# Pooled attention and squared-ReLU feed-forward on one core: chunk 1's softmax in another layout, another weight conversion, and split products in half of chunk 0

## The chip, the cores and the metric

The kernel runs on one NeuronCore of a Trainium2 chip. Its inputs lie in the chip's memory (HBM) and its result is written there. The metric is the device time of one execution in microseconds (us). The engines named below are PE (TensorE: matmuls and transposes by a matmul with an identity; PEld is its weight loading), DVE (VectorE), ACT (ScalarE), POOL (GpSimd) and SP (SyncE, which here only issues DMAs). Each engine works through its own queue in order.

## The reference

Keys and values are pooled over 8 tokens, each of the 8 batches and 8 heads attends over 72 pooled tokens, and the result, seen as 4608 tokens of width 512, goes through two weight matrices with a squared ReLU between them.

```python
def _attn_ref(q, k, v):                       # 8 batches, 8 heads, 576 tokens, head size 64
    k_p = k.reshape(B, H, Sp, 8, D).mean(axis=3)          # Sp = 72
    v_p = v.reshape(B, H, Sp, 8, D).mean(axis=3)
    scores = scale * np.matmul(q, k_p.transpose(0, 1, 3, 2))
    scores = scores - np.max(scores, axis=-1, keepdims=True)
    attn = np.exp(scores)
    attn = attn / (np.sum(attn, axis=-1, keepdims=True) + 1e-09)
    return np.matmul(attn, v_p).astype(np.float32)
...
    x = attn_out.transpose(0, 2, 1, 3).reshape(B * S, H * D)     # 4608 x 512
    h = np.maximum(x @ w_in, 0.0)                                # 512 x 2048
    return (h * h @ w_out).astype(np.float32)                    # 2048 x 512
```

The two weight matrices come as 64-bit floats, q, k and v as 32-bit floats.

## The kernel before

The 4608 tokens are cut into 12 chunks of 384 (`CH`), numbered c. Chunk 0 lies within batch 0; chunk 1 takes 192 tokens from batch 0 and 192 from batch 1 (`segments`). For each chunk there are 16 steps, one for each block of 128 columns of the hidden layer (`fc`). `hidden(c, fc)` multiplies the chunk's attention output x by a block of w_in (tile `h`), `project(c, fc)` multiplies the squared ReLU by a block of w_out and sums over all 16 blocks in three PSUM banks (tile `o`). `project` runs two steps behind `hidden` (`LAG`).

Products are made in one of two ways. From chunk 1 on every operand is split into a high and a low part in the type fp32r (`split`: ACT rounds to the high part, DVE subtracts), and three products of such parts replace one product of 32-bit floats: 12 matmuls for a block of `h`. In chunk 0 the weights are not yet split, and plain 32-bit floats are multiplied: 4 matmuls for a block of `h`, and the trace shows two records for each.

The weights are converted on the chip from the two 32-bit words of a 64-bit float. One weight piece (`key`, 512 KB of 64-bit values) is loaded into a `raw` tile by `land`. `magnitude` lets ACT take the absolute value of the high words into a half tile `wf`. `to_float32` then lets DVE do four instructions on 128x512 elements for each key: a clamp, a shift with a mask, and two that bring in sign and low bits. `split_weights` later makes the split pair `wt` for chunk 1 and all that follow. There are 32 keys.

Attention goes by pairs of heads p (four pairs a chunk). `transpose_q` turns q (tile `qps`, copied to `st`), `scores` multiplies with the pooled keys (tile `sps`, copied to `sc`). In chunk 1 and later the scores lie with the 72 pooled tokens on the partitions, so maximum and sum run across partitions: GpSimd does them with `partition_all_reduce` (tiles `mx` and `tot`), the sums travel to HBM and back (`send_sums`, `fetch_sums`), DVE inverts them, and the reciprocals travel once more (`rd`, `rb`). `weigh_values` multiplies with the pooled values (tile `av`). Chunk 0 is done with the tokens on the partitions: `token_scores`, `token_normalise` (DVE reductions, tiles `tm` and `te`) and `token_turn`, which transposes the weights back (tile `pps`).

Before step 0 stands a part written out by hand: it pools the keys of batches 0 and 1 (`pool_k`), pools values with a matmul against a matrix of ones (`pool_v_pair`, tile `vps`, copied to `vp`), and does all of chunk 0's attention. After it, the table `work` says which function runs in which step; `at(step, f, ...)` fills it. `EARLY` holds the steps for chunk 1's pairs, `STEADY` for the later ones. In a step the order is: `hidden`, the PE part of that step's attention functions, `project`, then the rest for ACT and DVE, the weight conversions, and last the activation of the `h` block just made. All DMAs are issued by SP in program order; each one also waits on one of eight semaphores taken in turn, so that a DMA is issued only when the eighth one before it has landed.

Three PSUM banks (`ps_a`) serve the tiles `qps`, `sps`, `kps`, `vps` and `av`; two (`ps_h`) serve `h`, and three (`ps_o`) the sums `o`.

Of the kernel before, what the change touches and what calls it, by code (L numbers as in the profile page):

```python
# [10 lines left out]
F32 = mybir.dt.float32  # L11
F32R = mybir.dt.float32r
U32 = mybir.dt.uint32
AF = mybir.ActivationFunctionType
ALU = mybir.AluOpType
AX = mybir.AxisListType
EXP_MIN = 2.0 ** -15
EXP_MAX = 122879.9921875
# [14 lines left out]
def pooled_attn_relu2_ffn(  # L33
# [38 lines left out]
    IDLE = (3, 1)  # L72
# [9 lines left out]
    EARLY = ((-19, -16, -13, -10), (0, 2, 3, 5, 5, 6, 7, 8))  # L82
# [14 lines left out]
    make_identity(nc, ident)  # L97
# [43 lines left out]
    def magnitude(key):  # L141

        words = raw[key].rearrange("p a (n w) -> p a n w", w=2)
        wf[key] = half_tile("f", "wf_" + "_".join(map(str, key)))
# [112 lines left out]
    def pool_v_pair(b, p):  # L257
# [6 lines left out]
        def then():  # L264
            DVE.tensor_copy(kv[b][2][:, 2 * p:2 * p + 2, :].rearrange("s h d -> s (h d)"), pt[:SP_, :2 * D])
# [49 lines left out]
    def scores(c, p):  # L315
# [3 lines left out]
        early = c == 1  # L319
        if early:  # L320

            blocks = st.rearrange("p (i t s) -> p i t s", i=2, s=QT)
            for i in range(2):
                h = 2 * p + i
                for t, (b, _, _) in enumerate(segments(c)):
                    for two in range(2):
                        rows = slice(two * D, (two + 1) * D)
                        PE.matmul(ss[two][:SP_, (i * 2 + t) * QT:(i * 2 + t + 1) * QT], lhsT=kf[b][rows, h // KH, h % KH * SP_:(h % KH + 1) * SP_],
                                  rhs=blocks[rows, i, t, :], start=True, stop=True)
        else:  # L330
# [374 lines left out]
```

## Time and profile before

| | us |
|---|---|
| median of 3 runs (lowest, highest) | 972.17 (971.12, 972.57) |
| the profiled execution | 971.68 |
| its span, first to last instruction | 969.9 |
| PE busy (98% of the span) | 946.1 |
| DVE busy (65%) | 628.5 |
| ACT busy (44%) | 428.3 |
| POOL busy (41%) | 394.1 |

The time is the span plus 1.8 us around it. Times of day in this text (such as "at 43.83") are us from the start of the span. In the rows of the timeline the first number is the start, the second how long the group lasted up to its last end; since matmuls overlap, the pace of PE is read from one start to the next. In the rows of the stages the number ahead of the comma is the length of the stage, and then come busy time and count for each engine.

### The profile page before, as it was taken

The numbers are of one execution on the slowest core, as the hardware profiler recorded it, in microseconds if no ns is written. First come the engines' busy times: TensorE is split into PE (matmuls) and PEld (weight loads), VectorE is DVE, ScalarE is ACT, GpSimd is POOL, SyncE is SP. The second block draws the span as 40 slices with busy tenths as digits, with TensorE's granted clock in tenths as the row PEclk, the third lists the DMA queues.
The fourth block names the chain that finished last, engine by engine and source line by source line (L and its number), as shares of the span: only waits on it lengthen the run. The fifth ranks groups of instructions, "written<-read, shape, count | busy, mean of one in ns | idle before, by whom it ended". The sixth has DMA issues, their size and how long they took to land.

```text
span 969.9 us, 13344 instructions
## 1 busy us (share of the span) xinstructions
PE 946.1 (98%) x4888; PEld 793.5 (82%) x4888; DVE 628.5 (65%) x1034; ACT 428.3 (44%) x847; POOL 394.1 (41%) x209
## 2 busy tenths in 40 slices
PE   5989899999999999999999999999999999999998
PEld 5644457888888888888888888888888888888997
DVE  4869997877765556767775656667776555453221
ACT  1644466774434445344444434443543434432322
POOL 4288733544344443443434335343534534440000
PEclk9999999999999999999999999999999999999999
DMA  9926212112211112112112102102311210100000
GB/s 239 365 95 217 82 34 66 48 52 87 60 45 62 38 38 70 34 51 92 54 39 76 37 20 78 52 30 52 95 52 30 77 32 18 58 10 9 33 1 32
DMA packets 53361, 64.45 MB, mean 66 GB/s; under 512 B 14936, under 2 KB 34480, under 8 KB 53296
## 3 DMA queue, kind: packets, MB, share of 16 engines
q1 hardware_dynamic: 53296, 63.61, 21.4%
q8 instruction: 38, 0.62, 0.3%
q14 instruction: 27, 0.22, 0.1%
HBM read 53.87 MB, written 9.71 MB: 66 GB/s over the span
## 4 chain that ended last, share of the span: by engine, by line
PE 85%; DVE 8%; issue 3%; DMA 2%; ACT 1%; POOL 0%; SPq 0%; DVEq 0%; POOLq 0%
PE o L29 38%; PE h L29 37%; PE av L29 4%; PE sps L29 3%; DVE wf_o L29 2%; DVE wf_i L29 2%; PE qps L29 1%; PE vps L29 1%; DMA q<-in_q_dram 1%; DMA rd<-rr 0%; DVE st L29 0%; PE kps L29 0%; DVE sc L29 0%; DVE kp L29 0%; POOL tot L29 0%
## 5 line engine op out<-in xcount | busy, mean ns | idle before, releaser
L29 PE MATMUL h<-xh,w_i 128*128 128x384 f32 x1408 | 389.1, 337 | 0.0
L29 POOL PARTITION_ALL_REDUCE tot<-sc x88 | 250.1, 2889 | 217.8 <-issue 201.6
L29 PE MATMUL o<-w_o,gh 128*128 128x512 f32 x1056 | 335.2, 398 | 0.4 <-ACT ob L29 0.4
L29 PEld LDWEIGHTS h<-xh,w_i 128*128 128x128 f32 x1408 | 258.7, 188 | 8.5 <-issue 0.5
L29 PE MATMUL h<-xl,w_i 128*128 128x384 f32 x704 | 238.0, 338 | 0.0
L29 PEld LDWEIGHTS o<-w_o,gh 128*128 128x128 f32 x1056 | 192.6, 188 | 52.1 <-issue 15.3
L29 POOL PARTITION_ALL_REDUCE mx<-sc x88 | 131.4, 1540 | 243.6 <-ACT sc L29 243.6
L29 DVE TENSOR_TENSOR gl<-r,gh 128x384 fp32r<-128x384 f32 x176 | 146.5, 832 | 108.4 <-ACT gh L29 106.5
L29 PE MATMUL o<-w_o,gl 128*128 128x512 f32 x528 | 208.7, 395 | 0.0
L29 DVE TENSOR_TENSOR r<-r 128x384 f32<-128x384 f32 x160 | 105.7, 661 | 108.7 <-ACT r L29 108.3
L29 ACT CAST gh<-r 128x384 fp32r<-128x384 f32 x176 | 90.4, 514 | 150.1 <-DVE r L29 149.6
L29 PEld LDWEIGHTS h<-xl,w_i 128*128 128x128 f32 x704 | 132.2, 188 | 8.1 <-issue 0.7
L29 ACT ACTIVATE r<-h 128x384 f32<-128x384 f32 x192 | 93.8, 488 | 99.9 <-PE h L29 98.6
L29 PEld LDWEIGHTS o<-w_o,gl 128*128 128x128 f32 x528 | 99.1, 188 | 22.5
L29 DVE TENSOR_TENSOR st<-qps,st 64x384 fp32r<-64x384 f32 x80 | 60.3, 754 | 48.1 <-ACT st L29 47.2
L29 ACT CAST st<-qps 64x384 fp32r<-64x384 f32 x80 | 59.4, 742 | 52.6 <-PE qps L29 52.0
L29 ACT ACTIVATE sc<-sc 72x384 f32<-72x384 f32 x88 | 43.7, 525 | 70.1 <-DVE sc L29 70.1
L29 ACT CAST xh<-rb 128x384 fp32r<-128x384 f32 x44 | 22.6, 513 | 108.5 <-DVE rb L29 108.5
L29 DVE TENSOR_REDUCE vp<-v 72x64 f32<-72x512 f32 x48 | 51.0, 1063 | 0.0
L29 DVE TENSOR_REDUCE kp<-k 96x64 f32<-96x512 f32 x42 | 43.7, 1041 | 3.4 <-DMA k<-in_k_dram 3.4
L29 DVE TENSOR_TENSOR sc<-sc,mx 72x384 f32<-72x384 f32 x88 | 44.6, 546 | 0.0
L29 PE MATMUL av<-sc,vp 72*64 72x384 f32 (+1 forms) x256 | 43.1, 425 | 0.9 <-ACT sc L29 0.9
(82 smaller groups left out, 701.8 us busy)
## 6 DMA issues: line engine op xcount, KB each, us to landing
k<-in_k_dram SPq DMA_DIRECT2D x48, 192.0 KB
out_dram<-ob SPq DMA_DIRECT2D x36, 256.0 KB
rb<-rd SPq DMA_DIRECT2D x88, 96.0 KB
raw_i<-in_moe_w_in_dram SPq DMA_DIRECT2D x16, 512.0 KB
raw_o<-in_moe_w_out_dram SPq DMA_DIRECT2D x16, 512.0 KB
v<-in_v_dram SPq DMA_DIRECT2D x48, 144.0 KB
q<-in_q_dram SPq DMA_DIRECT2D x30, 192.0 KB
q<-in_q_dram SPq DMA_DIRECT2D x32, 96.0 KB
```

Of the source, the lines that this page charges most:

```text
L29: return lambda *a, **k: self.tc.keep_in_program_order(f(*a, **k))
```

## The change

It has several parts, all of which concern the time before step 0, chunk 0 and the attention of chunk 1:

- `EARLY`: chunk 1's softmax is done like chunk 0's, with `token_scores`, `token_normalise` and `token_turn`. For chunk 1 the exponentials are read by ACT straight from PSUM, in eight instructions a pair, each with its own bias.
- Weights: ACT also converts a 16-bit part of the low word into the bits to be added, in place in the `raw` tile, and DVE does three instructions a key.
- `SPLIT = 8`: blocks 0 to 7 of chunk 0 use plain products as before; blocks 8 to 15 use split parts of x (`split_x0`) and split w_in, whose `split_weights` moves into chunk 0.
- The identity for transposes is built by DVE with ramps and comparisons (before: by GpSimd). `keep_busy` issues 16 matmuls before the first transposes and 2 later (before: 3 and 1).
- The copies of `vps` go from DVE to ACT.
- The loads are reordered, and batch 1's value pairs 2 and 3, the transposes of batch 1's keys and chunk 1's first q and scores move from the part ahead of step 0 into steps 0 to 3.

```diff
-EXP_MIN = 2.0 ** -15
-EXP_MAX = 122879.9921875
+SHIFT = 2.0 ** 16
+EXP_MIN = 2.0 ** -15 * SHIFT
+EXP_MAX = 122879.9921875 * SHIFT
+LOW = 7.4999 / 65535
...
-    IDLE = (3, 1)
+    IDLE = (16, 2)
...
-    FIRST, EAGER, AHEAD = 2, 8, 5
+    FIRST, EAGER, AHEAD = 2, 10, 4
+    SPLIT = 8
...
-    EARLY = ((-19, -16, -13, -10), (0, 2, 3, 5, 5, 6, 7, 8))
+    EARLY = ((-16, -13, -10, -7), (0, 1, 2, 3, 4))
...
-    make_identity(nc, ident)
+    ramp = const.tile([P, 2, 32], F32, name="ramp")
+    DVE.memset(ident, 0.0)
+    DVE.memset(ramp[:, 0, :1], 0.0)
+    for n in (1, 2, 4, 8, 16):
+        DVE.tensor_scalar(ramp[:, 0, n:2 * n], ramp[:, 0, :n], float(n), None, op0=ALU.add)
+    DVE.transpose(ramp[:, 1, :], ramp[:, 0, :])
+    for n in range(0, P, 32):
+        rows = slice(n, n + 32)
+        DVE.tensor_scalar(ident[rows, rows], ramp[rows, 0, :], ramp[rows, 1, :1], None, op0=ALU.is_equal)
...
-        ACT.activation(wf[key].rearrange("p (a n) -> p a n", a=2), words[..., 1].bitcast(F32), AF.Abs)
+        ACT.activation(wf[key].rearrange("p (a n) -> p a n", a=2), words[..., 1].bitcast(F32), AF.Abs, scale=SHIFT)
+        halves = raw[key].bitcast(U16).rearrange("p a (n w) -> p a n w", w=4)
+        ACT.activation(words[..., 0], halves[..., 1], AF.Copy, scale=LOW)
...
             DVE.tensor_scalar(m, m, EXP_MIN, EXP_MAX, op0=ALU.max, op1=ALU.min)
-        for _, _, m in parts:
-            DVE.tensor_scalar(m, m, 3, 0x3FFFFFF8, op0=ALU.logical_shift_left, op1=ALU.bitwise_and)
         for words, _, m in parts:
-            DVE.scalar_tensor_tensor(m, words[..., 1], 0xC0000000, m, op0=ALU.bitwise_and, op1=ALU.bitwise_or)
+            DVE.scalar_tensor_tensor(m, m, 3, words[..., 0], op0=ALU.logical_shift_left, op1=ALU.bitwise_or)
         for words, _, m in parts:
-            DVE.scalar_tensor_tensor(m, words[..., 0], 29, m, op0=ALU.logical_shift_right, op1=ALU.bitwise_or)
+            DVE.scalar_tensor_tensor(m, words[..., 1], 0x80000000, m, op0=ALU.bitwise_and, op1=ALU.bitwise_or)
...
-            DVE.tensor_copy(kv[b][2][:, 2 * p:2 * p + 2, :].rearrange("s h d -> s (h d)"), pt[:SP_, :2 * D])
+            ACT.copy(kv[b][2][:, 2 * p:2 * p + 2, :].rearrange("s h d -> s (h d)"), pt[:SP_, :2 * D])
...
     def token_scores(c, p):
-        ss = [ps_o.tile([P, 512], F32, name=f"sps_{c}_{p}_{j}", tag=f"o{(2 * p + j) % NTT}") for j in range(2)]
+        ss = token_banks(c, p, "sps", "o")
...
+                if c:
+                    DVE.tensor_scalar(m[:, 1, i], m[:, 0, i], -SCALE, None, op0=ALU.mult)
...
+                for t in range(NQ if c else 0):
+                    ACT.activation(e[i][:, t], views[i][:, t], AF.Exp, bias=m[:, 1, i, t:t + 1], scale=SCALE)
...
+    def split_x0():
+        xts[0] = [sb.tile([P, NPAIR, CH], F32R, name=f"{x}_0", tag=x, bufs=2) for x in ("xh", "xl")]
+        for i, x in enumerate(x0):
+            split(*(t[:, 2 * i:2 * i + 2] for t in xts[0]), x)
...
-            if c == 0:
-                prods += [(wf[key][:, cols], xts[c][:, cc, :])]
+            if c == 0 and fc < SPLIT:
+                prods += [(wf[key][:, cols], x0[cc // 2][:, cc % 2, :])]
             else:
                 prods += [(wt[key][:, w, cols], xts[c][x][:, cc, :]) for w, x in ((0, 0), (0, 1), (1, 0))]
...
+    load_q(1, 0)
...
-    for key in first_keys:
+    for key in keys[:FIRST + 2]:
         land(key)
+    for p in range(NPAIR):
+        load_v_pair(1, p)
...
-        after = [token_scores(0, p + 2)] if p + 2 < NPAIR else []
-        after.append(pool_v_pair(1, p))
+        after = [token_scores(0, p + 2), pool_v_pair(1, p)] if p + 2 < NPAIR else []
...
-        transpose_k(1, hf)()
+        at(0, transpose_k, 1, hf)
         at(9 + hf, split_k, 1, hf)
+    for p in range(2, NPAIR):
+        at(p, pool_v_pair, 1, p)
+    at(3, split_x0)
...
-        at(14 + int(i * 0.48), split_weights, key, DVE)
+        if key[0] == "i" and key[1] * WC >= SPLIT * P:
+            at(need[key] + 1, split_weights, key, DVE)
+        else:
+            at(14 + int(i * 0.48), split_weights, key, DVE)
```

The first place where the order changes is SP's queue ahead of step 0. Before, batch 1's values (`vv_0` to `vv_3`, the second set) follow the last keys of batch 1 (`k_4`) at once:

```order
L29 DMA k_4_95<-in_k_dram 96x512 x2
L29 DMA vv_0_96<-in_v_dram 96x2x384
L29 DMA vv_1_97<-in_v_dram 96x2x384
L29 DMA vv_2_98<-in_v_dram 96x2x384
L29 DMA vv_3_99<-in_v_dram 96x2x384
L29 DMA raw_i_0_100<-in_moe_w_in_dram 128x2x512
L29 DMA raw_i_2_101<-in_moe_w_in_dram 128x2x512
L29 DMA raw_o_102<-in_moe_w_out_dram 128x1024
L29 DMA raw_i_0_103<-in_moe_w_in_dram 128x2x512
```

In the changed kernel, on the same queue, two loads of chunk 1's q and four weight pieces stand between them:

```order
L34 DMA k_4_104<-in_k_dram 96x512 x2
L34 DMA q_0_105<-in_q_dram 96x2x128 x2
L34 DMA raw_i_0_106<-in_moe_w_in_dram 128x2x512
L34 DMA raw_i_2_107<-in_moe_w_in_dram 128x2x512
L34 DMA raw_o_108<-in_moe_w_out_dram 128x1024
L34 DMA raw_i_0_109<-in_moe_w_in_dram 128x2x512
L34 DMA vv_0_110<-in_v_dram 96x2x384
L34 DMA vv_1_111<-in_v_dram 96x2x384
L34 DMA vv_2_112<-in_v_dram 96x2x384
L34 DMA vv_3_113<-in_v_dram 96x2x384
```

Six DMAs moved ahead of `vv_0`, and nothing else in that stretch.

The second place is PE ahead of step 0. Before, the four poolings of batch 1's values (`vps` from the second `vv` set), the `pps` transposes and the `av` products alternate down to the keys of batch 1 (`kps`):

```order
L29 MATMUL vps_1_356<-vv_1_97,ones 72x128 x6
L29 MATMUL av_0_364<-sc_0_328,vp_154 64x384 x2
L29 MATMUL pps_1_0_368<-ident,te_1_228 72x96 x4
L29 MATMUL pps_1_1_369<-ident,te_1_228 72x96 x4
L29 MATMUL vps_2_396<-vv_2_98,ones 72x128 x6
L29 MATMUL av_1_403<-sc_1_378,vp_154 64x384 x2
L29 MATMUL pps_2_0_410<-ident,te_2_332 72x96 x4
L29 MATMUL pps_2_1_411<-ident,te_2_332 72x96 x4
L29 MATMUL vps_3_430<-vv_3_99,ones 72x128 x6
L29 MATMUL av_2_437<-sc_2_420,vp_154 64x384 x2
L29 MATMUL pps_3_0_441<-ident,te_3_382 72x96 x4
L29 MATMUL pps_3_1_442<-ident,te_3_382 72x96 x4
```

In the changed kernel the same stretch of PE goes on to the first block `h_0` without poolings 2 and 3:

```order
L34 MATMUL vps_1_387<-vv_1_111,ones 72x128 x6
L34 MATMUL av_0_396<-sc_0_359,vp_186 64x384 x2
L34 MATMUL pps_1_0_400<-ident,te_1_259 72x96 x4
L34 MATMUL pps_1_1_401<-ident,te_1_259 72x96 x4
L34 MATMUL av_1_428<-sc_1_410,vp_186 64x384 x2
L34 MATMUL pps_2_0_437<-ident,te_2_363 72x96 x4
L34 MATMUL pps_2_1_438<-ident,te_2_363 72x96 x4
L34 MATMUL av_2_456<-sc_2_447,vp_186 64x384 x2
L34 MATMUL pps_3_0_460<-ident,te_3_414 72x96 x4
L34 MATMUL pps_3_1_461<-ident,te_3_414 72x96 x4
L34 MATMUL av_3_479<-sc_3_470,vp_186 64x384 x2
L34 MATMUL h_0_514<-x_0_394,wf_i_0_432 128x384 x2
```

Two poolings left the stretch; `vps_0` and `vps_1` stay where they were, ahead of `pps_0` and of `av_0`.

The third place is ACT behind the last copy of x (`x_363`, now `x_1_395`). Before, the keys, the q and two weight pieces follow:

```order
L29 COPY x_363<-av_3_463 128x384
L29 COPY kf_467<-kps_0_468 128x288
L29 COPY kf_467<-kps_1_473 128x288
L29 COPY st_0_489<-qps_0_484 128x384
L29 ACTIVATE wf_o_495<-raw_o_102 128x512
L29 ACTIVATE wf_o_495<-raw_i_0_103 128x512
L29 COPY sc_0_512<-sps_0_0_502 72x2x192
```

In the changed kernel, behind the same copy on ACT, ten weight instructions come first:

```order
L34 COPY x_1_395<-av_3_479 128x384
L34 ACTIVATE wf_o_483<-raw_o_108 128x512
L34 ACTIVATE raw_o_108<-raw_o_108 128x512
L34 ACTIVATE wf_i_0_486<-raw_i_0_109 128x512
L34 ACTIVATE raw_i_0_109<-raw_i_0_109 128x512
L34 ACTIVATE wf_i_0_486<-raw_i_2_114 128x512
L34 ACTIVATE raw_i_2_114<-raw_i_2_114 128x512
L34 ACTIVATE wf_o_483<-raw_o_115 128x512
L34 ACTIVATE raw_o_115<-raw_o_115 128x512
L34 ACTIVATE wf_o_498<-raw_o_116 128x512
L34 ACTIVATE raw_o_116<-raw_o_116 128x512
L34 COPY kf_519<-kps_0_520 128x288
```

The copies of `kf` and `st` moved behind five pieces of weights, and each piece takes two instructions instead of one.

More of the change, by code (lines that the diff above doesn't have):

```diff
@@ L7 @@
 from concourse import mybir
-from concourse.masks import make_identity
 from concourse._compat import with_exitstack
@@ L468, in then @@
             if c == 0:
-                ACT.copy(xts[c][:, p, :], av[:, :CH])
+                ACT.copy(x0[p // 2][:, p % 2, :], av[:, :CH])
                 return
             xh, xl = xts[c]
+            if c == 1:
+                split(xh[:, p, :], xl[:, p, :], av[:, :CH])
+                return
             DVE.tensor_tensor(rb, av[:, :CH], rb, op=ALU.mult)
@@ L555, in pooled_attn_relu2_ffn @@
         load_k(1, i)
-    for p in range(NPAIR):
-        load_v_pair(1, p)
+    load_q(1, 0)
     need = {}
```

95 lines of the change are left out of this document (43 added, 52 removed).

## The prediction

> **What bounds the kernel now.** I read the page first: PE is busy 98% of the span, so the time is PE's work and the stretches where PE waits.
>
> ```profile
> span 969.9 us, 13344 instructions
> PE 946.1 (98%) x4888; PEld 793.5 (82%) x4888; DVE 628.5 (65%) x1034; ACT 428.3 (44%) x847; POOL 394.1 (41%) x209
> ```
>
> Then the timeline of PE, to find the two marks between which the change acts: the first `h` of chunk 0 (43.83) and the first of chunk 1 (140.02). After 140 PE's order stays as it is, so what moves the second mark moves the end.
>
> ```profile
> 9.41 1.65 PE L29 MATMUL idle<-ident 128*128 128x128 f32 x6 [9.41 <-POOL ident masks.py:199]
> ...
> 24.62 0.90 PE L29 MATMUL sps<-kf,st 64*96 64x72 f32 x16 [0.24 <-ACT st L29]
> 25.45 1.53 PE L29 MATMUL vps<-vv,ones 96*72 96x128 f32 x12
> 26.82 0.82 PE L29 MATMUL pps<-ident,te 96*72 96x96 f32 x8
> 27.58 0.39 PE L29 MATMUL sps<-kf,st 64*96 64x72 f32 x2
> ...
> 28.99 1.53 PE L29 MATMUL vps<-vv,ones 96*72 96x128 f32 x12
> 30.45 0.87 PE L29 MATMUL av<-sc,vp 72*64 72x384 f32 x4
> 31.25 0.85 PE L29 MATMUL pps<-ident,te 96*72 96x96 f32 x8
> ...
> 41.26 0.71 PE L29 MATMUL kps<-ident,kp 96*128 96x96 f32 x6
> 41.90 0.55 PE L29 MATMUL qps<-ident,q 96*128 96x96 f32 x4
> 43.02 0.88 PE L29 MATMUL sps<-st,kf 64*72 64x96 f32 x16 [0.57 <-ACT st L29]
> 43.83 2.85 PE L29 MATMUL h<-x,wf_i 128*128 128x384 f32 x8
> ...
> 58.01 1.45 PE L29 MATMUL h<-x,wf_o 128*128 128x384 f32 x4
> ...
> 60.59 0.50 PE L29 MATMUL qps<-ident,q 96*128 96x96 f32 x4
> 60.92 2.77 PE L29 MATMUL o<-wf_i,r 128*128 128x512 f32 x6
> ...
> 99.58 2.74 PE L29 MATMUL o<-wf_i,r 128*128 128x512 f32 x6
> 102.15 1.45 PE L29 MATMUL h<-x,wf_o 128*128 128x384 f32 x4
> ...
> 140.02 0.73 PE L29 MATMUL h<-xh,w_i 128*128 128x384 f32 x1
> ```
>
> From start to start a plain `h` block takes 58.01 to 60.59, 2.58 us (two rows of four), an `o` step 2.57 (99.58 to 102.15), a pair's `av` 0.80. The chain of work that ended last has a split block of 12 matmuls at 2.10:
>
> ```profile
> 166.37 2.10 PE h L29 x12
> ```
>
> The stage between the marks (its length, then busy PE, PEld, DVE, ACT, POOL) and PE's longest waits in it:
>
> ```profile
> 43.83:140.02 96.19, 88.90 (x322) 46.00 (x321) 85.42 (x150) 49.05 (x97) 69.97 (x21) 1.00 0.38 123
> ```
>
> ```profile
> PE h L29 <- ACT r L29: 3.3, 2, 2.1
> PE h L29 <- DVE wf_i L29: 3.2, 4, 1.2
> ```
>
> DVE is busy 85.42 of 96.19 us: in chunk 0 PE waits for it, or for ACT, which had waited on it in turn. PE's own work there, at the paces above, is 16 x 2.58 of `h`, 14 x 2.57 of `o`, four `av` (0.8), five `qps` (0.33) and five `sps` (0.81): 41.3 + 36.0 + 3.2 + 1.7 + 4.0 = 86.2. The other 10.0 are 6.5 of these waits and 3.5 of shorter ones and joints between groups.
>
> **The change, part by part.**
>
> *Split products in blocks 8 to 15.* 2.58 less 2.10, eight times: PE saves 3.8 us.
>
> *Softmax of chunk 1.* Its scores cost PE the same 16 matmuls a pair; `pps` is new, 0.76 a pair (26.82 to 27.58), 3.0 us. The all-reduces leave POOL, and the exchange of sums leaves SP's queue. DVE takes reductions and two normalising passes instead.
>
> *Work moved behind the first mark.* `kps` (0.64), chunk 1's first `qps` (0.33) and `sps` (0.81) and two poolings (1.37 each, 25.45 to 26.82): 4.5 us. PE's work between the marks becomes 86.2 - 3.8 + 3.0 + 4.5 = 89.9.
>
> *Weight conversion.* The prices by kind and shape:
>
> ```profile
> L29 DVE TENSOR_SCALAR wf_i<-wf_i 128x512 uint32<-128x512 uint32 x16 | 9.7, 641 | 0.1
> ...
> L29 ACT ACTIVATE wf_o<-raw_o 128x512 f32<-128x512 f32 x9 | 6.1, 680 | 0.0
> ...
> L29 ACT COPY sc<-pps 72x384 f32<-72x384 f32 x8 | 6.2, 876 | 2.4 <-PE pps L29 2.4
> ...
> L29 ACT ACTIVATE te<-te 96x288 f32<-96x288 f32 x8 | 3.1, 437 | 7.2 <-DVE te L29 7.2
> ```
>
> DVE loses 32 shifts; the 16 of this row are 9.7 us. ACT gains 32 conversions of a 16-bit part, which the trace does not have. Lower bound: the magnitude's pace, 0.58 back to back (the second of the pair at 34.69 below). Upper bound: the scattered copy of `sc`, scaled to 512 (876 x 512/384 = 1.17 us). I take 0.58, since the stride is the magnitude's: 30 keys, 17 us, on an ACT that is busy 49 of 96. At 1.17 it gains 35 and is still not full.
>
> *Exponentials from PSUM.* Eight of 96x72 a pair; the nearest row is 96x288 at 437 ns, so 0.11 (by elements) to 0.44 each. I take 0.25, 2 us a pair, beside PE's `h`. [...]
>
> With DVE relieved I leave 1.0 us of the 6.5: behind the last copy of x, ACT has ten weight instructions (5.8) ahead of `kf` and `st`, while PE gets to chunk 1's first scores in 6.1; and the splits of w_in come just in time for block 12. Of the 3.5 I keep 3.0. Between the marks: 89.9 + 1.0 + 3.0 = 93.9.
>
> *Ahead of step 0.* What is late next is batch 1's values, now behind six other loads:
>
> ```profile
> 24.51 0.38 SPq L29 DMA_DIRECT2D raw_i<-in_moe_w_in_dram  x1
> ```
>
> ```profile
> 19.00:23.00 4.00, 3.63 (x40) 3.15 (x39) 2.14 (x7) 0.81 (x2) 3.67 (x9) 1.00 1.10 235
> 24.00:33.00 9.00, 8.53 (x91) 7.18 (x90) 8.58 (x25) 4.57 (x9) 3.43 (x8) 1.00 1.04 394
> ```
>
> ```profile
> raw_i<-in_moe_w_in_dram SPq DMA_DIRECT2D x10, 512.0 KB
> ...
> vv<-in_v_dram SPq DMA_DIRECT2D x8, 288.0 KB
> q<-in_q_dram SPq DMA_DIRECT2D x6, 96.0 KB
> ```
>
> (The stages' last column is GB/s: values come at 235, weights at 394.) SP issues a DMA when the eighth before it has landed, so the `raw_i` at 24.51 tells that batch 1's `vv_3` had; `vv_0` had three transfers earlier (0.88 MB, 3.8 us), at 20.7. Now two q (0.2 MB, 0.8 us) and four weight pieces (2.1 MB, 5.3) come first, and `vv_0` lands at 26.8. PE works in order: `pps_0` and all that follows it stand behind `vps_0`, which ran at 25.45 before and now starts at 26.8, so `pps_0` at 28.2. From there to the last copy of x the trace took 26.82 to 41.85, 15.0 us:
>
> ```profile
> 34.69 1.26 ACT L29 ACTIVATE wf_i<-raw_i 128x512 f32<-128x512 f32 x2
> ...
> 41.37 0.48 ACT L29 COPY x<-av 128x384 f32<-128x384 f32 x1 [0.95 <-PE av L29]
> ```
>
> To this come 1.1 for two more weight instructions on ACT in the middle of the chain, less 0.6 for a stop inside `sps_3` (27.58 to 28.99 is 1.41; the same work at 24.62 took 0.83). The copies of `vps` that move to ACT fit its waits there (2.4 for `pps`). The first `h` starts at 28.2 + 15.0 + 1.1 - 0.6 = 43.7. The identity from DVE and the 16 idle matmuls let PE begin near 3 instead of 9.41, but that ends in the wait for `vv_0`: costed at nothing.
>
> The sum (A): 43.7 + 93.9 = 137.6 against 140.02, 2.4 us less: 969.3 for the profiled execution (971.68), 969.8 on the median of 972.17, which lies 0.49 above it.
>
> **Rivals.**
>
> *B, the clock falls in the wait.* PE's pace nearly doubles in the middle of a row of like matmuls (poolings), and its granted clock falls after the end:
>
> ```profile
> 17.20:18.20 1.00, 1.00 (x6) 1.00 (x6) 0.00 (x0) 0.00 (x0) 0.92 (x4) 1.00 1.06 274
> 18.20:19.20 1.00, 1.00 (x11) 1.00 (x10) 0.00 (x0) 0.00 (x0) 0.92 (x2) 1.00 1.07 259
> 966.00:969.90 3.90, 0.13 (x1) 0.00 (x0) 0.00 (x0) 0.64 (x2) 0.00 (x0) 1.00 0.52 202
> 969.90:972.00 2.10, 0.00 (x0) 0.00 (x0) 0.00 (x0) 0.00 (x0) 0.00 (x0) 0.67 0.00 0
> ```
>
> Six matmuls a us became eleven; and some 4 us after the last matmul (966.1) the clock is down, 0.67 on average over the last 2.1 us. In the changed kernel PE stands still between `sps_2` (done between 20 and 23: 25.45 less what the early start brings) and 26.8. If these 4 to 7 us drop the clock, `vps_0` to `av_0` (25.45 to 31.25 here, some 5 us of matmuls) run at half pace, 4.5 us more, less 0.5 when the pace returns: 141.6, 973.3 (973.8 on the median). [...]
>
> *C, slower: the clock stays down until step 0*, since PE is thinly used after `av_0`. Then two `pps` and two `av` on the chain cost another 1.3, and the first blocks of `h` at half pace 2: 144.9, 976.6 (977.1). Against it: that in this trace PE, as thinly used before 43, kept its pace (the first eight `h` took 2.85).
>
> *D, ACT becomes the bound of steps 0 to 3.* If a 16-bit conversion costs 1.17, twenty of them put ACT 12 us behind, of which perhaps 4 reach PE: 973.3. Against it stands the stride.
>
> *E, the change doesn't do what it says:* the split blocks still wait on DVE, and 3.8 us come back as waits on `w_i`: 973. It has part of D's chance.
>
> **How the numbers follow.** A 0.47, B 0.25, C 0.18, D and E 0.10. The gap of B may miss the point at which the clock falls; hence not more for B and C. A measurement of this kernel tells 0.2% (1.9 us) from no change. With some 2 us of doubt on joints and chain A is faster by more in 0.34 of its 0.47, and B, D and E add 0.05: faster 0.39. Same: 0.12 of A, 0.14 of B, 0.04 of the others: 0.30. Slower: 0.31. The range goes from A without waits, with joints halved and a chain 0.5 shorter (965.8, rounded to 965.5), to C.
>
> **What would show it.** Chunk 1's first `h` near 137.6; `vps` waiting on the DMA of `vv` until 27; no PE wait on `wf_i`; PE's clock at 1.00 through that wait (A) or a dip behind it (B, C); 12 `h` matmuls in 2.1 us from block 8 on; POOL idle from 28 to 105. I am wrong if `vv_0` lands before 25, if the 16-bit conversion is far from 0.58, or if PE's waits on ACT's `r` pass 3 us.

## The result and the profile after

The changed kernel takes 979.15 us (median of 9 runs, 976.67 to 980.99), the kernel before 971.12 us in the same series (9 runs, 968.38 to 976.00). The ratio is 1.0076 with a 95% interval of 1.0054 to 1.0097: slower by 0.5 to 1.0%. The forecast was 969.8, with a range from 965.5 to 977.1; the median lies 2 us above the range.

The head of the page of the changed kernel (profiled execution 978.61 us):

```profile
span 976.9 us, 13532 instructions
PE 957.1 (98%) x4980; PEld 811.7 (83%) x4980; DVE 611.6 (63%) x1028; ACT 451.9 (46%) x913; POOL 332.9 (34%) x191
```

DVE lost 17 us of work and POOL 61, as the change says. PE is busy 11 us longer, though its products cost less: a sign of slower work, not of more. The timeline of PE shows where:

```profile
3.38 6.38 PE L34 MATMUL idle<-ident 128*128 128x128 f32 x32 [3.38 <-DVE ident L34]
...
21.23 0.90 PE L34 MATMUL sps<-kf,st 64*96 64x72 f32 x16
27.81 2.81 PE L34 MATMUL vps<-vv,ones 96*72 96x128 f32 x12 [5.67 <-DMA vv<-in_v_dram]
30.41 1.49 PE L34 MATMUL pps<-ident,te 96*72 96x96 f32 x8
...
36.08 1.55 PE L34 MATMUL av<-sc,vp 72*64 72x384 f32 x4
...
45.09 2.23 PE L34 MATMUL av<-sc,vp 72*64 72x384 f32 x4 [2.11 <-ACT sc L34]
...
51.23 5.45 PE L34 MATMUL h<-x,wf_i 128*128 128x384 f32 x8
56.52 0.67 PE L34 MATMUL kps<-ident,kp 96*128 96x96 f32 x6
57.35 2.77 PE L34 MATMUL h<-x,wf_i 128*128 128x384 f32 x8
...
146.59 0.74 PE L34 MATMUL h<-xh,w_i 128*128 128x384 f32 x1
```

PE now starts at 3.38 instead of 9.41, and stands still for 5.67 us ahead of `vps_0`. What follows takes twice as long: a pooling 2.81 (1.53 before), `pps` 1.49 (0.82), the first block of `h` 5.45 against 2.77 for the second. The first mark is at 51.23 (before 43.83), the second at 146.59 (before 140.02): 6.6 us of the 7.0 by which the span grew lie ahead of the second mark.

The granted clock says the same. In the trace's record it is full from 8.73 to 25.80, half until 56.52, then full until 974.70, behind the last matmuls. Stages cut at these times (length, then busy PE, PEld, DVE, ACT, POOL, and the clock behind them):

```profile
22.39:25.80 3.41, 0.00 (x0) 0.00 (x0) 3.24 (x10) 0.00 (x0) 3.10 (x9) 1.00 1.08 310
25.80:29.21 3.41, 1.40 (x7) 1.43 (x8) 0.34 (x1) 0.00 (x0) 1.96 (x5) 0.50 1.09 266
...
32.63:36.04 3.41, 3.41 (x22) 3.00 (x20) 2.52 (x7) 0.89 (x4) 0.00 (x0) 0.50 1.04 392
...
53.11:56.52 3.41, 3.41 (x7) 1.58 (x6) 3.38 (x7) 3.41 (x7) 0.00 (x0) 0.50 0.00 0
51.23:146.59 95.36, 93.17 (x436) 59.20 (x435) 76.51 (x152) 77.91 (x171) 10.04 (x5) 0.97 0.27 86
```

Behind the idle stretch of 3.41 us the clock is down, at 0.50. It stays down through 32.63 to 36.04, though PE is busy 3.41 of 3.41 there, and comes back at 56.52, behind a stretch filled by `h`.

Between the marks (the last row) nothing went wrong. PE's waits there are these three, 2.2 us in all; of before, the two longest rows alone made 6.5:

```profile
PE av L34 <- ACT te L34: 1.3, 1, 1.3
PE pps L34 <- DVE te L34: 0.7, 1, 0.7
PE h L34 <- ACT r L34: 0.2, 1, 0.2
```

And the 16-bit conversion on ACT, whose price the trace of before did not have (the groups by form: total, mean ns of one):

```profile
L34 ACT ACTIVATE raw_o<-raw_o 128x512 uint32<-128x512 uint16 x16 | 11.0, 686 | 0.0
```

The 686 ns include some overlap with the next; from start to start it is 0.56, as for the magnitude beside it. That ends rival D.

### The profile page after: what moved, and what is told of

Read it like the earlier page. It is cut to its first block, busy times and chain, and to the rows that moved or that the text cites. A ratio compares the mean times of both kernels' runs of the same rounds, so it can differ in the third digit from the quotient of the medians.

```text
span 976.9 us, 13532 instructions
## 1 busy us (share of the span) xinstructions
PE 957.1 (98%) x4980; PEld 811.7 (83%) x4980; DVE 611.6 (63%) x1028; ACT 451.9 (46%) x913; POOL 332.9 (34%) x191
## 3 DMA queue, kind: packets, MB, share of 16 engines
HBM read 53.08 MB, written 9.68 MB: 64 GB/s over the span
## 4 chain that ended last, share of the span: by engine, by line
PE 92%; DVE 2%; DMA 2%; ACT 2%; issue 1%; SPq 1%; ACTq 0%
PE o L34 41%; PE h L34 40%; PE av L34 4%; PE sps L34 3%; PE qps L34 1%; DMA vv<-in_v_dram 1%; PE vps L34 1%; DMA k<-in_k_dram 1%; DVE wf_o L34 1%; DVE wf_i L34 1%; DMA q<-in_q_dram 1%; PE pps L34 1%; SPq L34 1%; ACT raw_i L34 0%; DVE tm L34 0%
## 5 line engine op out<-in xcount | busy, mean ns | idle before, releaser
L34 PE MATMUL h<-xh,w_i 128*128 128x384 f32 x1472 | 411.8, 340 | 0.0
L34 PEld LDWEIGHTS h<-xh,w_i 128*128 128x128 f32 x1472 | 269.8, 188 | 10.1 <-issue 1.0
L34 POOL PARTITION_ALL_REDUCE tot<-sc x80 | 201.4, 2564 | 209.9 <-issue 199.5
L34 PE MATMUL h<-xl,w_i 128*128 128x384 f32 x736 | 247.2, 336 | 0.0
L34 POOL PARTITION_ALL_REDUCE mx<-sc x80 | 118.4, 1527 | 319.0 <-ACT sc L34 319.0
L34 DVE TENSOR_TENSOR gl<-r,gh 128x384 fp32r<-128x384 f32 x176 | 143.6, 816 | 109.0 <-ACT gh L34 108.7
L34 PEld LDWEIGHTS h<-xl,w_i 128*128 128x128 f32 x736 | 138.2, 188 | 10.1 <-issue 2.6
L34 ACT ACTIVATE sc<-sc 72x384 f32<-72x384 f32 x80 | 39.7, 525 | 46.4 <-DVE sc L34 46.4
L34 PE MATMUL av<-sc,vp 72*64 72x384 f32 (+1 forms) x256 | 46.4, 448 | 4.0 <-ACT sc L34 2.7
L34 PE MATMUL o<-wf_o,r 128*128 128x512 f32 x96 | 44.4, 598 | 0.0
```

Source lines behind the costliest of these rows:

```text
L34: return lambda *a, **k: self.tc.keep_in_program_order(f(*a, **k))
```

## The experiments

All kernels were profiled and timed against the kernel before, run beside them; the third column is the ratio to those runs. The kernel before has one median of its own in each of the series, from 970.32 to 972.59, so medians of different series are comparable only to some 2 us. The marks are read from the profiled executions, one of each kernel.

| run | median, us | ratio (95%) | first `h` | second mark |
|---|---|---|---|---|
| before | 971.12 | | 43.83 | 140.02 |
| changed | 979.15 | 1.0076 (1.0054 to 1.0097) | 51.23 | 146.59 |
| e1: values first | 967.61 | 0.9978 (0.9965 to 0.9991) | 39.89 | 134.83 |
| e2: wait bridged | 973.83 | 1.0044 (1.0028 to 1.0060) | 46.62 | 142.62 |
| e3: short warm-up | 979.71 | 1.0101 (1.0078 to 1.0124) | 52.42 | 147.81 |
| e4: before, values late | 981.64 | 1.0112 (1.0085 to 1.0139) | 49.54 | 146.71 |
| e5: e1, poolings back | 964.50 | 0.9949 (0.9927 to 0.9971) | 39.60 | 132.91 |
| e6: e1, first weights later | 965.46 | 0.9948 (0.9928 to 0.9969) | 38.38 | 134.45 |
| e7: e1, no split products | 970.08 | 1.0005 (0.9981 to 1.0029) | 39.82 | 136.94 |
| e9: e5 and e6 | 963.46 | 0.9907 (0.9882 to 0.9932) | 36.38 | 131.56 |
| e10: e9, last wait filled | 963.76 | 0.9933 (0.9905 to 0.9962) | 36.60 | 131.78 |
| e8: e9, old conversion | 968.54 | 0.9983 (0.9954 to 1.0012) | 35.92 | 134.13 |
| e11: e9, short warm-up | 974.49 | 0.9995 (0.9962 to 1.0028) | 49.35 | 142.09 |
| e12: e9, ReLU first | 960.42 | 0.9868 (0.9838 to 0.9898) | 36.63 | 128.89 |
| e13: bridge on 32 rows | 980.70 | 1.0087 (1.0053 to 1.0122) | 52.69 | 148.68 |
| e14: dense work behind the wait | 980.65 | 1.0092 (1.0060 to 1.0124) | 54.12 | 149.50 |

**e1, the load order undone.**

```diff
     for i in range(NKT):
         load_k(1, i)
+    for p in range(NPAIR):
+        load_v_pair(1, p)
     load_q(1, 0)
...
     for key in keys[:FIRST + 2]:
         land(key)
-    for p in range(NPAIR):
-        load_v_pair(1, p)
```

> The changed kernel with batch 1's four value loads put back in SP's queue directly behind the keys of batch 1, ahead of chunk 1's q and the four weight pieces; nothing else. Theory W (the late load makes PE stand still, the standstill halves its clock, and this is the whole loss): vv_0 has landed when sps_2 is over (22.1), so vps_0 follows at once, pps_0 at 23.5, no dip of the clock behind 20; 15.5 us of chain at full pace give a first h of chunk 0 near 39.0 (51.23 in the changed kernel); between the marks 95.4 less the 2.7 that its first h block lost at half pace, 92.7; second mark 131.7, 14.9 us earlier, so some 962 to 964 us. Theory L (the wait costs its length of 5.7 us, and the clock falls anyway because PE is thinly used by the small work ahead of step 0): first h near 45.5, clock at half until after it, second mark near 141, some 973 us. Theory K (the weights, now later by some 4 us, make step 0 wait instead): PE waits for wf_i or for ACT ahead of the first h, first h at 43 or later, clock at 1.00.

PE's timeline, and two stages cut at the clock's times:

```profile
22.01 1.53 PE L34 MATMUL vps<-vv,ones 96*72 96x128 f32 x12
...
30.16 0.85 PE L34 MATMUL pps<-ident,te 96*72 96x96 f32 x8
33.74 2.25 PE L34 MATMUL av<-sc,vp 72*64 72x384 f32 x4 [2.73 <-ACT sc L34]
...
39.89 4.07 PE L34 MATMUL h<-x,wf_i 128*128 128x384 f32 x8
```

```profile
28.74:32.15 3.41, 2.27 (x12) 0.95 (x12) 3.21 (x11) 3.17 (x8) 0.00 (x0) 1.00 1.04 398
32.15:35.56 3.41, 1.82 (x4) 0.58 (x4) 3.15 (x7) 2.23 (x4) 0.00 (x0) 0.50 1.05 395
```

The wait on the DMA is gone and `vps_0` runs at 22.01. Theory W holds for the loads: this one order is worth 11.8 us of span (976.9 to 965.1), and with it the change is faster than the kernel before. But W had also expected no fall of the clock behind 20, and 962 to 964 us. The clock falls again, at 32.15, in the middle of another wait, 2.73 us for ACT's copy of `sc`, and the time is 967.61.

**e2, the same late loads, but PE kept at work.**

```diff
-        after = [token_scores(0, p + 2), pool_v_pair(1, p)] if p + 2 < NPAIR else []
+        after = [token_scores(0, p + 2)] if p + 2 < NPAIR else []
+        if p == 0:
+            keep_busy(24)
+        if p + 2 < NPAIR:
+            after.append(pool_v_pair(1, p))
```

> The changed kernel with 24 further matmuls of the identity (some 4.9 us at full clock) between the scores of pair 2 and the pooling of batch 1's first values, so that PE works through most of its wait for vv_0; the loads stay as they are in the changed kernel. Theory W: the wait of some 5.7 us remains as lost time, but the clock stays at 1.00; vps_0 at 27.8, pps_0 at 29.2, first h near 44.7, second mark near 137.4, some 969 to 970 us, so about 9 us less than the changed kernel; the difference to the kernel with values loaded first is then the wait alone (5 to 6 us). Theory L (clock falls in the thin work behind the wait): clock at half from about 30, first h near 50, second mark near 145, 977 us or more.

```profile
22.46 5.62 PE L34 MATMUL idle<-ident 128*128 128x128 f32 x48
28.76 1.50 PE L34 MATMUL vps<-vv,ones 96*72 96x128 f32 x12 [0.68 <-DMA vv<-in_v_dram]
...
40.46 2.24 PE L34 MATMUL av<-sc,vp 72*64 72x384 f32 x4 [2.75 <-ACT sc L34]
```

Matmuls that compute nothing make the kernel 5.3 us faster. `vps_0` comes 0.95 us later than in the changed kernel (28.76), runs at full pace, and the first `h` comes 4.6 earlier: the half clock behind the wait cost at least 5.6 us ahead of the first mark (at least, since e2 itself is at half clock from 40.26 on). The wait by itself is what is left of the distance to e1: at `vps_0` 5.8 us in the changed kernel (27.81 against 22.01) and 6.7 in e2. W's 969 to 970 was missed for the same reason as in e1: a second fall, here at 40.26, behind the same wait for ACT.

**e3, the old warm-up** (`IDLE = (3, 1)` instead of `(16, 2)`).

> The changed kernel with the old number of idle matmuls at the start (3 and 1 instead of 16 and 2); the loads stay as they are in the changed kernel. Theory W: without the early start PE runs at half pace until about 18, as in the kernel before, and reaches the wait for vv_0 some 3 to 4 us later (25 to 26 instead of 22.1); the standstill shrinks to about 2 us, too short to halve the clock; vps_0 still at 27.8, first h near 44.7 and some 969 to 970 us. Fewer idle matmuls then make the kernel faster by 9 us. Rival M (the early idle matmuls do only good): PE comes later to everything ahead of the wait, the clock falls in the wait or is never full ahead of it, first h at 51 or later, 979 us or more.

```profile
28.97 2.81 PE L34 MATMUL vps<-vv,ones 96*72 96x128 f32 x12 [3.69 <-DMA vv<-in_v_dram]
```

Rival M was right. PE arrives 3.1 us later (25.3), the standstill is 3.69, not 2, and the clock still falls. The time is that of the changed kernel: its early start is worth nothing as long as `vv_0` is late.

**e4, the late values alone, in the kernel before.**

```diff
-    for p in range(NPAIR):
-        load_v_pair(1, p)
...
-    for key in first_keys:
-        land(key)
-    for key in keys[FIRST:EAGER]:
+    for key in keys[:FIRST + 2]:
+        land(key)
+    for p in range(NPAIR):
+        load_v_pair(1, p)
+    for key in keys[FIRST + 2:EAGER]:
         land(key)
```

> The kernel before with one edit: four weight pieces instead of none stand in SP's queue ahead of batch 1's values (chunk 1's q stays where it was). Theory W: vv_0 lands at some 26.5 to 27.5 instead of ahead of 25.45, PE stands still for 1 to 2 us there, too short for the clock to fall; first h near 45 to 46 (43.83 before), and the time is 1 to 2 us longer than before (0.1 to 0.2%). Rival N (any wait at this place drops the clock): first h at 49 or later, 6 us or more longer. Rival O (values needed no earlier): no difference.

```profile
29.95 2.81 PE L29 MATMUL vps<-vv,ones 96*72 96x128 f32 x12 [7.02 <-DMA vv<-in_v_dram]
```

W's size was wrong, and N came out: a wait of 7.02 us, a fallen clock, first `h` at 49.54, span 976.6 (+6.7). In this execution PE was at full clock from 13.31 (18.29 in the profile of before) and so was early, and `vv_0` late. The times spread from 975.63 to 984.92, so the 11 us between the medians are no better known than that. What it shows: four weight loads ahead of the values cost the old kernel as much as the whole change did.

**e5 and e6, two ways to shorten the second wait.** e5 puts poolings 2 and 3 back; e6 moves four weight instructions on ACT.

```diff
 # e5, on e1
-        after = [token_scores(0, p + 2), pool_v_pair(1, p)] if p + 2 < NPAIR else []
+        after = [token_scores(0, p + 2)] if p + 2 < NPAIR else []
+        after.append(pool_v_pair(1, p))
...
-    for p in range(2, NPAIR):
-        at(p, pool_v_pair, 1, p)
 # e6, on e1
-        if p == 2:
-            for key in first_keys:
-                magnitude(key)
         token_turn(0, p)()
+        if p >= 2:
+            magnitude(first_keys[p - 2])
...
-    to_float32(*first_keys)
+    for key in first_keys:
+        to_float32(key)
```

> The kernel of the first experiment (values loaded first) with one more edit: poolings 2 and 3 of batch 1's values go back from steps 2 and 3 to their places in chunk 0's attention, behind pps_2 and pps_3. Theory P (the second dip, from 32.15 to 42.39 in the first experiment, comes from a wait of 2.7 us for ACT that nothing fills any more since the poolings moved away): the wait ahead of av_2 shrinks to some 1.3 us, the clock stays at 1.00; first h near 38.6 (39.89), its block takes 2.6 to 2.8 (4.07), steps 2 and 3 lose 2 x 1.4; some 4 to 5 us less than the first experiment, near 963. Rival Q (poolings ahead of step 0 are on the chain and cost what they save): first h near 41 to 42, no gain over the first experiment, 967 to 968.

> The kernel of the first experiment (values loaded first) with one more edit: the four weight instructions of the first two keys, which stand on ACT ahead of the copies of sc for pair 2, go behind the copies of sc, one key behind pair 2's and one behind pair 3's. Theory R (these four instructions, 2.2 us, make the wait of 2.7 us that halves the clock a second time): the wait ahead of av_2 falls to about 0.6 us, no dip; first h near 36.9 (39.89), its block 2.6 to 2.8 instead of 4.07; 4 us less than the first experiment, 963 to 964. Rival S (the weights then end the chain): PE waits for wf_i ahead of the first h, first h at 39 or later, and the clock falls there; no gain, 967 or more.

Of e5, the waits on PE's timeline; of e6, the stage ahead of its fall:

```profile
34.45 1.58 PE L34 MATMUL av<-sc,vp 72*64 72x384 f32 x4 [1.47 <-ACT sc L34]
...
37.45 2.22 PE L34 MATMUL av<-sc,vp 72*64 72x384 f32 x4 [0.64 <-ACT sc L34]
```

```profile
28.64:32.05 3.41, 2.35 (x13) 1.02 (x12) 3.21 (x12) 3.15 (x8) 0.26 (x1) 1.00 1.04 389
```

Each is faster than e1, by 3.1 and 2.2 us at the median, and in each the clock fell all the same: at 37.05 in e5 and 32.05 in e6. P and R named the right waits (1.47 against an expected 1.3; 0.65 against 0.6) but took it that a wait must be long, and so the times of 963 to 964 that they expected were missed. In e6 no wait in that stretch is longer than 0.65; together they leave PE 2.35 busy of 3.41, and the clock falls.

**e7, plain products in all of chunk 0** (e1 with `SPLIT = 16` and no `split_x0`).

> The kernel of the first experiment (values loaded first) with plain products in all 16 blocks of chunk 0 (SPLIT = 16, without the split of chunk 0's x). By the prediction's term each of the blocks 8 to 15 takes 2.58 instead of 2.10: 8 x 0.48 = 3.8 us more than the first experiment, 971 to 972. Rival: with fewer splits on ACT and DVE in chunk 0 other waits vanish, or the splits of w_in later crowd chunk 1, so that the difference is under 2 us or over 6.

2.5 us at the median (its twelve times spread from 968.61 to 977.82) and 2.1 at the second mark, not 3.8. The wait of block 2 on ACT's `r`, 1.6 us in e1, is 0.4 here: 2.1 and 1.2 make 3.3 of the 3.8, and a third of it comes back as that wait; why ACT is later there was not followed up.

**e9 and e10, both edits, and the last wait filled.**

```diff
 # e10, on e9
+    t = ps_o.tile([P, 512], F32, name="fill", tag="o2")
+    for _ in range(3):
+        PE.matmul(t[:, :P], lhsT=ident, rhs=ident, start=True, stop=True)
     weigh_values(0, NPAIR - 1)()
```

> The two edits of the last experiments together, on the kernel with values loaded first: poolings 2 and 3 back in chunk 0's attention, and the first weight instructions on ACT behind the copies of sc. Theory U (the clock falls when the waits within one window of 3.4 us add up to some 1.15 us or more, as in the windows in which it fell at 32.15, 37.05 and 32.05 in the three kernels, and stays when they add up to 0.7 or less): poolings fill the waits ahead of av_1 and av_2, 0.65 us ahead of av_3 is left, no dip ahead of step 0; av_2 near 33.0, first h near 37.6, its block 2.6 to 2.8; second mark some 4 us earlier than with the poolings alone, 960 to 961 us. Theory V (a fall needs no particular wait; this thin work loses the clock somewhere in any case): a dip of two or three windows before 45, first h near 38.5 to 39.5, 963 to 965 us.

> As the run with both edits, with three matmuls of the identity (0.6 us) in PE's wait ahead of av_3. Theory U: if that run has no dip ahead of step 0, this makes no difference (within 1 us); if it has one, it goes here, and this is 3 us faster. Theory V: the same dip and the same time.

e9, PE's timeline and the stage ahead of its first fall:

```profile
34.90 1.54 PE L34 MATMUL av<-sc,vp 72*64 72x384 f32 x4 [0.66 <-ACT sc L34]
36.38 3.23 PE L34 MATMUL h<-x,wf_i 128*128 128x384 f32 x8
...
43.78 0.90 PE L34 MATMUL sps<-kf,st 64*96 64x72 f32 x16 [0.74 <-ACT st L34]
46.43 4.51 PE L34 MATMUL h<-x,wf_i 128*128 128x384 f32 x8 [1.74 <-ACT r L34]
```

```profile
42.99:46.40 3.41, 0.95 (x17) 0.76 (x16) 3.38 (x8) 3.38 (x8) 0.00 (x0) 1.00 1.05 358
```

U holds ahead of step 0: one wait of 0.66, no fall, first `h` at 36.38, earlier than expected. Filling that wait (e10) changes nothing at the median, as U said; three of e10's twelve times lie near 972, none of e9's six. The time is 963.46, not 960 to 961: between waits of 0.74 and 1.74 on ACT in steps 1 and 2 the clock falls, at 46.40. So V's time came (963 to 965), but not the place that V gave for the fall.

**e8, the old conversion in e9.**

> As the run with both edits, with the weight conversion of the kernel before: one instruction on ACT and four on DVE for each key instead of two and three. By the prediction's terms ACT loses 30 x 0.57 = 17 us and DVE gains 30 x 0.6 = 18 us ahead of the second mark; DVE was full in chunk 0 before. Theory X (the conversion is what keeps PE from waiting in chunk 0): waits of PE on wf_i or on r of 2 to 5 us come back in chunk 0, and the time is 2 to 5 us longer. Rival Y (the softmax off the exchange and the splits already leave DVE enough room): no such waits, within 1 us, or faster by up to 1 us since ACT is free ahead of step 0.

PE's waits in e8, then the same two in e9:

```profile
PE av L34 <- ACT te L34: 3.6, 1, 3.6
...
PE h L34 <- ACT r L34: 2.6, 1, 2.6
...
PE h L34 <- DVE wf_i L34: 0.5, 1, 0.5
```

```profile
PE h L34 <- ACT r L34: 1.7, 1, 1.7
PE av L34 <- ACT te L34: 1.3, 1, 1.3
```

5.1 us slower at the median, 2.6 at the second mark: X's time came, and its waits came in part. Those for `r` and `wf_i` grow from 1.7 to 3.1; more comes from a wait that X did not name, of chunk 1's `av` for `te` (1.3 to 3.6). Where the part behind the second mark arises was not followed up. In this kernel the three-instruction conversion pays.

**e11, the old warm-up in e9** (`IDLE = (3, 1)`).

> The run with both edits (poolings back, first weights later, values loaded first) with the old number of idle matmuls at the start, 3 and 1. With the values late the warm-up made no difference to the time (979.71 against 979.15). Theory W: there its gain ended in the wait for vv_0; with the values early the gain reaches the end. PE then stands at half pace until about 18 again, reaches vps_0 3 us later (25.3 instead of 22.2), first h near 39.5 instead of 36.4, some 966 to 967 us against 963.5. Rival: another wait (DVE's te, ACT's sc) takes it up, under 1 us of difference.

Two waits on PE's timeline, and two stages cut at the clock's times:

```profile
19.91 1.53 PE L34 MATMUL vps<-vv,ones 96*72 96x128 f32 x12 [1.04 <-ACT vp L34]
...
22.34 0.90 PE L34 MATMUL qps<-ident,q 96*128 96x96 f32 x4 [0.57 <-ACT st L34]
```

```profile
18.95:22.36 3.41, 1.89 (x17) 1.70 (x17) 2.52 (x7) 1.24 (x4) 3.17 (x7) 1.00 1.13 274
22.36:25.77 3.41, 3.41 (x25) 3.06 (x26) 0.97 (x3) 0.80 (x3) 3.17 (x8) 0.50 1.06 340
```

W expected 3 us; it is 11 at the median. Nine of the twelve times lie between 973.96 and 977.04, three between 963.68 and 964.45: one kernel, two groups of times. In the profiled execution, one of the nine, the clock fell at 22.36 and stayed down to 53.08, though all four poolings stand there. Both waits (1.04 for `vp`, 0.57 for `st`) lie in one stretch there, with PE busy 1.89 of 3.41. In e9, cut every 3.413 us from 8.86 on, they lie in two, 15.68 to 19.10 and 19.10 to 22.51, with PE busy 2.38 and 2.84, and the clock stayed at 1.00.

That this divides the two groups of e11 is the author's estimate, not shown: one execution was traced. In six of the nine long ones the mean granted clock is 0.982 to 0.984, as in the traced one; in the three longest (976.09 to 977.04) it is 0.996 to 0.999, and what made these long is open. (The mean leaves out the time before the clock's first rise: it is 1.000 for the kernel before, whose clock rose at 18.29. A late first rise would look like this.) A few long executions with a low clock stand in other kernels too: two of twelve in e5 and three in e10, near 972, at 0.983 to 0.985.

**e12, ACT does the block's ReLU ahead of the weights in steps 0 to 3.**

```diff
         for f in later:
             f()
+        if activate and s < 4:
+            activate()
+            activate = None
```

> The run with both edits, and in steps 0 to 3 ACT does the squared ReLU of the block just made ahead of that step's weight instructions. Theory U: PE's waits of 0.74 and 1.74 us in steps 1 and 2, which together halved the clock at 46.40, shrink to 0.7 us together, the clock stays at 1.00 there, second mark some 2 to 3.5 us earlier, 960 to 961.5 us. Rival Z (the weights are then late by the two instructions of each block): PE waits on DVE for wf_i or wf_o in steps 2 to 6, and the time is the same within 1 us.

```profile
44.05 0.90 PE L34 MATMUL sps<-kf,st 64*96 64x72 f32 x16 [0.76 <-ACT st L34]
44.88 2.85 PE L34 MATMUL h<-x,wf_i 128*128 128x384 f32 x8
```

The wait of 1.74 is gone and so is the fall at 46.40, as U said. One short fall is left, from 98.37 to 101.78, behind a wait of 1.4 us for chunk 1's `te`; e9 has it too, from 101.02. 960.42 us (960.04 to 960.91) is the fastest of all, 1.0 to 1.6% under the kernel before.

**e13 and e14, the bridge on 32 rows, and dense work behind the wait.** Busy time does not order the stretches seen so far: the clock fell behind one with PE busy 2.37 of 3.41 us (e5, 33.64 to 37.05) and stayed behind one with 2.15 (e3, 113.46 to 116.87). With PE's time weighted by the rows that each matmul uses, out of 128, the two come to 0.44 and 0.47 of the stretch (last section). e13 varies the rows of the bridge alone; e14 puts dense work behind the wait.

```diff
 # e13, on e2
-    def keep_busy(n):
+    def keep_busy(n, rows=P):
...
-            PE.matmul(t[:, :P], lhsT=ident, rhs=ident, start=True, stop=True)
+            PE.matmul(t[:, :P], lhsT=ident[:rows, :], rhs=ident[:rows, :], start=True, stop=True)
...
-            keep_busy(24)
+            keep_busy(24, 32)
 # e14, on the changed kernel
         after = [token_scores(0, p + 2), pool_v_pair(1, p)] if p + 2 < NPAIR else []
+        if p == 0:
+            keep_busy(16)
```

> The changed kernel with the bridge of 24 identity matmuls in the wait for vv_0, as in the second experiment, but each on 32 rows of the array instead of 128; they take PE as long. Theory F (what counts in a stretch of 3.413 us is the time of PE's matmuls weighted by the rows that they use, of 128: in the runs so far it fell at 0.44 or less and stayed at 0.47 or more): the bridge weighs 0.25, so the clock falls inside it, one to two stretches after its start (25 to 30), although PE is busy without a gap; vps_0 takes 2.8 us, first h at 51 to 53, 978 to 981 us. Theory G (PE's busy time counts, or only gaps): the clock stays through the bridge as with 128 rows, vps_0 in 1.5 us, first h near 46.6, some 974 us.

> The changed kernel with 16 identity matmuls on 128 rows directly behind vps_0, where the clock is down. Theory F (the half clock lasted 30.7 us because the small products behind the wait use 64 to 96 rows and weigh under 0.75 of a stretch): a stretch filled by these matmuls brings full clock back at the first or second boundary behind them, between 32 and 38 instead of at 56.52; 16 further matmuls of 0.2 to 0.4 us take 4.5 to 6 us, pps_0 starts at 35 to 37, and from there the chain runs at full pace until the wait of 2.7 us ahead of av_2, where it falls again; first h at 51 to 53, no gain, 978 to 981 us. Theory G (the return needs time, not weight): the clock stays down to the first block of h, first h near 57 to 58, 984 us or more.

e13, PE's timeline (the operands behind the tiles begin with rows times columns) and two stages cut at the clock's times; then two stages of e14:

```profile
21.89 7.41 PE L34 MATMUL idle<-ident 32*128 32x128 f32 x48
29.23 2.84 PE L34 MATMUL vps<-vv,ones 96*72 96x128 f32 x12
```

```profile
22.02:25.43 3.41, 3.41 (x31) 3.41 (x32) 3.24 (x10) 0.00 (x0) 3.10 (x8) 1.00 1.05 335
25.43:28.84 3.41, 3.41 (x18) 3.41 (x17) 0.49 (x1) 0.00 (x0) 2.12 (x5) 0.50 1.10 267
```

```profile
32.61:36.02 3.41, 3.41 (x18) 3.41 (x18) 0.00 (x0) 0.00 (x0) 0.00 (x0) 0.50 1.03 398
36.02:39.43 3.41, 3.41 (x41) 3.20 (x41) 0.17 (x1) 1.32 (x3) 0.00 (x0) 1.00 1.05 401
```

The clock did what theory F expected in both. The bridge of 32 rows keeps PE busy 3.41 of 3.41 us and the clock falls inside it, at 25.43; with the bridge on 128 rows (e2, 23.19 to 26.60, busy 3.41 as well) it stayed at 1.00. And in e14, behind a stretch filled by matmuls on 128 rows, the clock is back at 36.02 (56.52 in the changed kernel). It falls again at 46.26 in the wait of 2.74 us ahead of `av_2`, and the 16 matmuls take 5.4 us, so nothing is gained in time. F's first `h` at 51 to 53 was missed (54.12): `vps_0` waited for its values until 29.56 here, 1.8 us later than in the changed kernel.

## Why the prediction was wrong, step by step

The forecast of the second mark was 137.6, and it came at 146.6. Term by term:

| term of the sum | forecast | measured | off by |
|---|---|---|---|
| `vv_0` lands | 26.8 | 27.8 | +1.0 |
| from there to the start of `av_0` | 4.4 | 8.3 | +3.8 |
| from `av_0` to the first `h` | 12.5 | 15.2 | +2.7 |
| the first block of `h` | 2.6 | 5.3 | +2.7 |
| the rest between the marks | 91.3 | 90.1 | -1.2 |

The step that failed is the sum behind the wait: "The first `h` starts at 28.2 + 15.0 + 1.1 - 0.6 = 43.7" goes on from `vps_0` at full pace, and so puts what the wait does to PE's pace at nothing. The place of the wait was right, and its end was right within 1.0 us. But it was priced by its length alone; e2 shows the other part, at least 5.6 us of half clock ahead of the first mark, and the first block of `h` took another 2.7 (5.3 instead of 2.6). Rival B named it, and its 4.0 for the stretch to `av_0` measured 3.8. That PE's early start "ends in the wait for `vv_0`: costed at nothing" held (e3).

The second failure is the argument against C, that PE "as thinly used before 43, kept its pace". Keeping the full clock was not the same as getting it back: in the changed kernel the clock stayed at 1.00 behind a stretch with PE busy 2.37 of 3.41 us (15.56 to 18.97), and once at 0.50 it did not come back behind one with 3.41 (32.63 to 36.04). So C is what happened, at a larger size: 2.7 instead of 1.3 on the chain, 2.7 instead of 2 for the blocks of `h`, and 1.0 for `vv_0`. The range ended at C's 977.1, 2 us short.

The poolings are a third point. In the kernel before, poolings 2 and 3 stood in that stretch and filled waits for ACT; the change takes them away. The prediction counted them as work moved behind the first mark, and did not ask what their going uncovers. With the values early it shows: without the poolings PE waits 2.73 us ahead of `av_2` and the clock falls (e1); with them alone it still falls (e5), with them and the weight instructions moved it stays (e9). In the changed kernel itself they would hardly have saved the clock: e11 has them, and its half clock, once there, lasted 30.7 us as well.

What the traces bear out: DVE and ACT (a 16-bit conversion 0.56 from start to start, forecast 0.58; eight small exponentials 1.76 a pair, forecast 2), and waits of 2.2 between the marks against 1.0 plus joints. Between the marks, without the half clock, the change gains what was forecast and 1.2 us more. The split alone is worth 2.1 to 2.5 of its 3.8 (e7), and the conversion pays (e8). E is out: PE's waits between the marks name no `w_i`, and with the loads in the old order the change is faster (e1). Two smaller errors bore on nothing here. By its own steps the lower end of the range is 969.8 - 1.0 - 1.5 - 0.5 = 966.8, not 965.8. And the copies of `vps` do not all fit ACT's waits: PE waits 1.04 us for one (0.37 before, on DVE), which the changed kernel loses again in the wait for `vv_0`, and which is one of the two waits behind e11's fall.

The length of a single gap does not tell these falls. At 25.80 the clock fell in a gap of 5.67 us. But in the stretches ahead of the falls at 32.05 in e6 and 22.36 in e11 no gap is longer than 0.65 and 1.04 us, and in that ahead of 25.43 in e13 there is none.

Not tried by themselves: the new softmax of chunk 1, the identity built by DVE, and the copies of `vps` on ACT.

## What to carry to other kernels

When an edit delays a transfer that PE waits for in order, price the wait twice: its length (here 5.8 us at `vps_0`, the changed kernel against e1), and what the work behind it costs at half clock until the full clock is back (here at least 5.6 us ahead of the first mark, e2). Before moving small matmuls out of a latency-bound stretch, look whether they fill waits there (ahead of `av_2` PE waited 2.73 us without the poolings, in e1, and 1.47 with them, in e5). Speeding PE up ahead of a fixed arrival only widened the gap here: 5.67 us with the long warm-up, 3.69 with the short one (e3), and the same time.

## What the runs showed of the hardware that was not expected

In the traces the granted clock reads 1.00 or 0.50. Fourteen runs (before, changed, e1 to e12) were cut into stretches of 3.413 us, up to 196 us and more, from 18.29 on in the kernel before and from 6.21 to 17.89 on in the others; each stretch shows one of the two values, none a mean between them. In the changed kernel the clock changes at 8.73, 25.80, 56.52 and 974.70: 5, 9 and 269 such stretches apart. In the kernel before it changes at 18.29 and 970.61, 279 stretches apart. So where they begin differs from run to run. That fits the two groups of times in e11, but is not shown to cause them, and three of its long executions show no long half clock.

Some of these stretches, with PE's busy time and the author's estimate of its share weighted by rows: each matmul record up to the start of the next, times its rows out of 128, from the timelines of PE.

| run | stretch | PE busy, us of 3.41 | share by rows | clock in it | clock behind it |
|---|---|---|---|---|---|
| changed | 22.39 to 25.80 | 0.00 | 0.00 | 1.00 | 0.50 |
| e13 | 22.02 to 25.43 | 3.41 | 0.25 | 1.00 | 0.50 |
| e11 | 18.95 to 22.36 | 1.89 | 0.41 | 1.00 | 0.50 |
| e5 | 33.64 to 37.05 | 2.37 | 0.44 | 1.00 | 0.50 |
| e3 | 113.46 to 116.87 | 2.15 | 0.47 | 1.00 | 1.00 |
| e1 | 15.08 to 18.49 | 2.37 | 0.48 | 1.00 | 1.00 |
| changed | 15.56 to 18.97 | 2.37 | 0.50 | 1.00 | 1.00 |
| changed | 32.63 to 36.04 | 3.41 | 0.70 | 0.50 | 0.50 |
| e11 | 25.77 to 29.19 | 3.42 | 0.72 | 0.50 | 0.50 |
| changed | 49.69 to 53.11 | 3.42 | 0.80 | 0.50 | 0.50 |
| e4 | 30.38 to 33.79 | 3.41 | 0.75 | 0.50 | 1.00 |
| changed | 53.11 to 56.52 | 3.41 | 1.00 | 0.50 | 1.00 |
| e14 | 32.61 to 36.02 | 3.41 | 1.00 | 0.50 | 1.00 |

By busy time alone the falls and the stretches that kept the clock overlap in this table, by rows they do not. The stretches that brought the clock back are apart from those that did not, but for the one of 0.80, which stays unexplained. In the changed kernel's attention PE works with `sps` on 64 rows, `av` on 72 and `vps` and `pps` on 96, and the half clock lasted 30.7 us. That the few rows are why is the author's estimate, which e14 fits. Rows were varied alone only in e13, columns alone in no run, and why rows should count is not shown.
